# Last layer of a fused attention, expert and token-mixing kernel: ten of twelve row blocks transposed by VectorE from 512-byte gathers instead of by TensorE

## The chip, the cores and the metric

The kernel runs on one core of a Trainium2 chip. The metric is device time in microseconds (us) of one execution, lower is better. The engines are named as the profile names them: PE is TensorE (PEld its weight loads), DVE is VectorE, ACT is ScalarE, POOL is GpSimd and SP is the engine that only issues transfers.

## The reference

Three layers follow one another on a batch of 2, 768 tokens and 512 channels: windowed attention with 8 heads, a layer with 8 experts in which each token goes to one expert, and a token-mixing layer. The change concerns the way from the second layer's rows into the third layer, which computes:

```
def _moe2_ref(x, w_theta, w_tok_r, w_tok_i, w_ch):
    theta = x @ w_theta
    cos_t, sin_t = (np.cos(theta), np.sin(theta))
    zr = x * cos_t
    zi = x * sin_t
    yr = np.einsum('ts,bsd->btd', w_tok_r, zr)
    yi = np.einsum('ts,bsd->btd', w_tok_i, zi)
    y = yr + yi
    u = x + y
    return u + np.maximum(u @ w_ch, 0.0)
```

Here x is what the expert layer gives: for token s, `p[e] * (relu(x[s] @ w1[e]) @ w2[e])`.

## The kernel before

**Expert layer.** Tokens are sorted by expert into 18 slots of 128 rows. The results of a slot leave PSUM scaled (`y_rows`, and `y_last` for the last full slot, `y_few` for the last partial one) into the DRAM table `yd`, one row of 512 channels (2 KB) for each token. The index `yidx` says for each token in which row of `yd` it lies.

**Last layer.** The 1,536 tokens are 12 blocks of 128, k = 0 to 11; blocks 0 to 5 are batch entry 0. The matrix products run as three products of split operands (high and low parts), so each operand is needed twice. For a block k:

- `gather_y(k)`: POOL issues an indirect transfer (a gather) of the block's 128 rows of `yd` into the tile `yg`, tokens on partitions, for which there are four buffers.
- `h_tr(k)`: PE transposes `yg` in four 128x128 pieces into a PSUM tile `b` (channels on partitions). `h_xh` copies it on ACT into `xh` and again into `xTf`, which the end of the layer needs; `h_xl` subtracts on DVE, which gives `xl`.
- `h_theta(k)`: 12 matmuls from `xh` and `xl` with the weights `wth` give theta, in PSUM tile `th`.
- `trig_a`, `trig_s`: theta is reduced to a small angle (`kk`, `rr`) and its sine and cosine are taken, on ACT and DVE. `trig_b` multiplies them with the gathered rows (`si` on POOL, `kk` on DVE). `trig_c` splits the products into the tiles `z` (copies on ACT, one difference on POOL, one on DVE).
- `h_mix(k, d)`, d = 0 to 3: 12 matmuls each from `z` with the token-mixing weights `wtok` (`wtokr` for all but the first block of an entry), accumulated in the PSUM tiles `a`.

Block 0 goes another way: its rows are gathered before the last slot is there, and `first_put` adds that slot's rows through a second matmul with a 0/1 matrix (`hitT`); then come theta(0), a transpose back, and `y_few`'s 32 matmuls into the tile `few`.

**Order.** Everything is issued in a hand-written order, each engine works its own list in order. Block 0 to 2 are woven by hand; from k = 1 the loop runs, and in its step k PE does h_mix(k, 0), theta(k+2), the transposes of block k+3, h_mix(k, 1), h_mix(k, 2), h_mix(k, 3):

```
            h_mix(k, 0)
            gather_y(k + 4)
            ...
            h_theta(k + 2)
            h_tr(k + 3)
            h_mix(k, 1)
            ...
            trig_a(k + 2)
            h_xh(k + 3)
            trig_s(k + 2)
            h_xl(k + 3)
```

Between these, `job_tick` works off pieces of a job list, one job in a step, on DVE and ACT: table weights that arrive as 64-bit floats are turned into 32-bit ones with integer operations (`jw`, lines 402 to 414). After the last block of an entry, `h_u` adds the mixing result onto `xTf`, `h_split` splits it and `h_out` does the product with `w_ch`.

Of the kernel before, what the change touches and what calls it, by code (L numbers as in the profile page):

```python
# [12 lines left out]
I32 = mybir.dt.int32  # L13
# [35 lines left out]
YLAST = RBASE[E - 1] * 128  # L49
NRAW = 3  # L50
# [35 lines left out]
HU = 32  # L86
XL = 0
# [8 lines left out]
def f32(ap):  # L96
    return ap.bitcast(F32)


@with_exitstack  # L100
def kernel(
# [93 lines left out]
    yidx = ct([128, NB], I32, "yidx")  # L195
    erows = {}
# [249 lines left out]
    with ExitStack() as actx:  # L446
# [338 lines left out]
        def lead_out():  # L785
            A.activation(y0, head["y"], AF.Copy)
# [582 lines left out]
    with ExitStack() as mctx:  # L1369
# [64 lines left out]
        def first_put():  # L1434

            outs = first["xT"] = [pB.tile([128, 2, 128], F32, tag="b", name="first") for _ in range(2)]
            for n, (rows, pick) in enumerate(((first["rows"], ident), (first["yo"], first["hitT"]))):
                for j in range(4):
                    PE.matmul(
                        outs[j // 2][:, j % 2],  # L1440
                        lhsT=rows[:, j * 128 : (j + 1) * 128],
                        rhs=pick,
                        start=(n == 0 and j % 2 == 0),
                        stop=(n == 1 and j % 2 == 1),
                    )
# [109 lines left out]
        def mm2_few(u, out=None):  # L1555
# [33 lines left out]
        def y_rows(r, lo, hi):  # L1589
            for i in range(lo, hi):  # L1590
# [6 lines left out]
                A.activation(yo[:P, :W], yp[:P, :W], AF.Copy, scale=ps)  # L1597
# [32 lines left out]
        for u in range(64):  # L1630
# [79 lines left out]
            if 0 <= i < RTILES[r]:  # L1710
                gather_p(r, i)
            if u == HU:
                gather_p0()
# [13 lines left out]
    with ExitStack() as hctx:  # L1727
        hb = hctx.enter_context(tc.tile_pool(name="hb", bufs=2, side="right", reuse_waits="tile"))
        pA = hctx.enter_context(tc.tile_pool(name="pA", bufs=6, space=PSUM))
        x2s, xTb, zs, xps, xparts, ths, trig, acc, us = {}, {}, {}, {}, {}, {}, {}, {}, {}  # L1730

        def gather_y(k):
            if k >= NB:
                return
            yg = hb.tile([128, DM], F32, tag="yg", name="yg", bufs=4)
            G.indirect_dma_start(yg, None, yd[:], bass.IndirectOffsetOnAxis(ap=yidx[:, k : k + 1], axis=0))
            x2s[k] = yg

        def h_tr(k, pool=None):
# [3 lines left out]
            if t == 0:  # L1743
                xTb[b] = hb.tile([128, 4, S], F32, tag="xTf", name="xTf")
            tp = (pool or pB).tile([128, 4, 128], F32, tag="a" if pool else "b", name="b")
            for j in range(4):
                PE.transpose(tp[:, j], x2s[k][:, j * 128 : (j + 1) * 128], ident)
            xps[k] = tp

        def h_xh(k, both=True):  # L1750
# [5 lines left out]
            if both:  # L1756
# [28 lines left out]
        def trig_a(k, c=slice(0, DM), tick=lambda: None):  # L1785
# [9 lines left out]
            V.tensor_scalar(kk, kk, MAGIC, None, op0=ALU.subtract)  # L1795
# [16 lines left out]
        def trig_i(k, c=slice(0, DM), eng=G):  # L1812
            if k < NB:
                si = trig[k][2][:, c]
                eng.tensor_tensor(si, si, x2s[k][:, c], op=ALU.mult)  # L1815

        def trig_r(k, c=slice(0, DM)):
            if k >= NB:
                return
            kk, x2 = trig[k][0][:, c], x2s[k][:, c]  # L1820
            V.tensor_scalar(kk, kk, -2.0, 1.0, op0=ALU.mult, op1=ALU.add)
            V.tensor_tensor(kk, kk, x2, op=ALU.mult)

        def trig_b(k, c=slice(0, DM), eng=G):
# [16 lines left out]
        def trig_c(k, c=slice(0, DM), eng=G):  # L1841
# [75 lines left out]
        for k in range(1, 4):  # L1917
            gather_y(k)
        halves = (slice(0, 256), slice(256, 512))
# [67 lines left out]
        gather_y(4)  # L1987
# [4 lines left out]
        for k in range(1, NB):  # L1992
# [10 lines left out]
            gather_y(k + 4)  # L2003
# [12 lines left out]
            if k == HS:  # L2016
                h_split(0, 0, 0, S)
                h_split(0, 1, 0, S, G)
# [10 lines left out]
            if k == HS:  # L2029
                h_split(0, 2, 0, S)  # L2030
                h_split(0, 3, 0, S, G)
# [72 lines left out]
```

## Time and profile before

| what | value |
|---|---|
| three runs, median (lowest to highest) | 473.17 us (472.94 to 473.29) |
| the profiled execution's own time | 472.97 us |
| its span, from first to last instruction | 471.2 us |
| PE busy | 462.9 us, 98% of the span |
| DVE busy | 349.4 us, 74% |
| ACT busy | 254.3 us, 54% |
| POOL busy | 134.0 us, 28% |

The last layer begins at about 290 us of the span. Of the span's own time 1.8 us lie around it. [...]

### The profile page before, as it was taken

How to read it: one execution, taken by the hardware profiler on the slowest of the kernel's cores; microseconds unless marked ns; L12 is line 12 of the kernel's file. 1: busy time of each engine (PE TensorE's matmuls, PEld its weight loads, DVE VectorE, ACT ScalarE, POOL GpSimd, SP SyncE). 2: the span in 40 equal slices, each digit the busy share in tenths (PEclk: the TensorE clock that was granted, in tenths of full speed). 3: DMA queues.
4: the chain of work that ended last, by engine and by line, in shares of the span. 5: the costliest groups of instructions: out<-in, count | busy, mean ns of one | idle time of the engine just before them, and what ended most of it. 6: DMA issues, size and time to landing. Idle time of an engine off the chain costs nothing.

```text
span 471.2 us, 9456 instructions
## 1 busy us (share of the span) xinstructions
PE 462.9 (98%) x3310; PEld 382.6 (81%) x3310; DVE 349.4 (74%) x918; ACT 254.3 (54%) x613; POOL 134.0 (28%) x185
## 2 busy tenths in 40 slices
PE   8999999999999999999999999999999999999996
PEld 4677777788888898878777888888888888888885
DVE  5888889778678687878887746587999899751522
ACT  5988786722647666565754544556555355520300
POOL 8602322204041403040514302104543332430400
PEclk9999999999999999999999999999999999999999
DMA  8977577616967888888999991600023000001022
GB/s 243 370 226 255 166 250 248 231 47 197 323 181 232 281 292 272 256 255 275 310 348 298 304 321 61 207 24 22 24 73 125 12 19 19 1 33 35 34 79 93
DMA packets 60490, 82.97 MB, mean 176 GB/s; under 512 B 5608, under 2 KB 39656, under 8 KB 60440
## 3 DMA queue, kind: packets, MB, share of 16 engines
q1 hardware_dynamic: 52212, 62.06, 40.3%
q0 software_dynamic: 4272, 9.92, 6.7%
q10 hardware_dynamic: 3956, 10.36, 6.6%
q8 instruction: 27, 0.44, 0.4%
q14 instruction: 23, 0.19, 0.1%
HBM read 70.94 MB, written 11.38 MB: 175 GB/s over the span
## 4 chain that ended last, share of the span: by engine, by line
PE 86%; ACT 4%; DMA 3%; issue 3%; DVE 3%; POOL 1%; DVEq 0%; ACTq 0%; POOLq 0%
PE a L1859 21%; PE o L1547 12%; PE h L1474 8%; PE h L1491 8%; PE b L1896 7%; PE th L1783 7%; PE s L557 4%; PE x L636 3%; PE pt L612 3%; PE o L1563 2%; ACT pr L589 2%; DMA yd<-yo 2%; PE y L653 1%; PE tr L1323 1%; PE small L860 1%
## 5 line engine op out<-in xcount | busy, mean ns | idle before, releaser
L1859 PE MATMUL a<-wtokr,z 128*128 128x512 f32 x480 | 85.9, 337 | 0.0
L1859 PEld LDWEIGHTS a<-wtokr,z 128*128 128x128 f32 x480 | 73.8, 188 | 9.3
L1547 PE MATMUL o<-w2s,hh 128*128 128x512 f32 x192 | 62.9, 407 | 0.0
L589 ACT ACTIVATE pr<-sm,st 128x256 f32<-128x256 f32 (+1 forms) x96 | 46.0, 482 | 15.4 <-DVE st L579 15.3
L1491 PE MATMUL h<-xT,w1s 128*128 128x288 f32 (+3 forms) x384 | 51.9, 284 | 1.2 <-DVE w1s L1352 0.7
L1491 PEld LDWEIGHTS h<-xT,w1s 128*128 128x128 f32 x384 | 48.8, 189 | 4.4 <-DVE w1s L1352 1.1
L1456 DVE TENSOR_TENSOR w2s<-raw,w2s 128x512 fp32r<-128x512 f32 x56 | 38.4, 688 | 8.4 <-ACT w2s L1455 8.4
L579 DVE CUSTOM_DVE_ANT_0 sm<-s,bias 128x256 f32<-128x256 f32 (+1 forms) x96 | 34.0, 395 | 9.2 <-PE s L557 5.1
L1474 PEld LDWEIGHTS h<-xT,raw 128*128 128x128 f32 x256 | 37.0, 190 | 4.4 <-issue 3.9
L1474 PE MATMUL h<-xT,raw 128*128 128x192 f32 (+3 forms) x256 | 40.5, 311 | 0.0
L1547 PE MATMUL o<-w2s,hl 128*128 128x512 f32 x96 | 38.0, 396 | 0.0
L1547 PEld LDWEIGHTS o<-w2s,hh 128*128 128x128 f32 x192 | 32.3, 184 | 6.2 <-DVE w2s L1456 1.6
L1455 ACT ACTIVATE w2s<-raw 128x512 fp32r<-128x512 f32 x56 | 35.0, 628 | 2.9 <-DMA raw<-in_w_dram 1.4
L1599 POOL DMA_DIRECT2D yd<-yo x13 | 8.3, 636 | 80.3 <-ACT yo L1597 80.3
L1904 DVE SCALAR_TENSOR_TENSOR ob<-b,xTf 128x512 f32<-128x512 f32 (+1 forms) x16 | 8.8, 556 | 27.1 <-PE b L1896 24.3
L1815 POOL TENSOR_TENSOR si<-si,yg 128x512 f32<-128x512 f32 x10 | 13.5, 1346 | 50.5 <-ACT si L1808 47.5
L1352 DVE TENSOR_TENSOR w1s<-raw,w1s 128x512 fp32r<-128x512 f32 x32 | 21.9, 688 | 5.9 <-ACT w1s L1351 4.5
L557 PE MATMUL s<-kall,q 64*128 64x256 f32 (+1 forms) x192 | 26.2, 393 | 0.0
L411 ACT ACTIVATE wtokr<-jw 128x512 fp32r<-128x512 f32 x15 | 9.5, 633 | 29.4 <-DVE jw L408 29.4
L404 DVE SCALAR_TENSOR_TENSOR jw<-jraw,jw 128x512 int32<-128x512 int32 x26 | 24.7, 952 | 0.4
L406 DVE SCALAR_TENSOR_TENSOR jw<-jraw,jw 128x512 int32<-128x512 int32 x26 | 24.6, 948 | 0.2
L612 PE MATMUL pt<-ident,pr 128*128 128x128 f32 x176 | 24.6, 278 | 0.1
(289 smaller groups left out, 968.9 us busy)
## 6 DMA issues: line engine op xcount, KB each, us to landing
raw<-in_w_dram SPq DMA_DIRECT2D x60, 512.0 KB, 5.2
vv<-in_pack_dram SPq DMA_DIRECT2D x10, 512.0 KB, 5.5
jraw<-in_w_tokT_dram ACTq DMA_DIRECT2D x10, 512.0 KB, 4.5
w<-in_w_dram SPq DMA_DIRECT2D x16, 256.0 KB, 6.0
kall<-in_pack_dram SPq DMA_DIRECT2D x10, 320.0 KB, 5.0
xd<-xt SPq DMA_DIRECT2D x12, 256.0 KB, 2.2
q<-in_pack_dram SPq DMA_DIRECT2D x11, 256.0 KB, 4.4
jraw<-in_w_tokT_dram ACTq DMA_DIRECT2D x10, 256.0 KB, 4.8
```

The lines of the kernel that those rows point to most:

```text
L557: PE.matmul(sp[hh][:, 0:W], lhsT=qs[n][half, j], rhs=kall[half, b, j, t * 160 + 160 - W : t * 160 + 160], start=True, stop=True,)
L579: V.tensor_tensor_reduce(out=sm[:, hh, 0:W], in0=ust[u]["s"][hh], in1=bias[:, 2 * j + hh], scale=-0.125, scalar=BIG, op0=ALU.add, op1=ALU.min,
L589: A.activation(pr[:, hh, 0:W], sm[:, hh, 0:W], AF.Exp, bias=st[:, hh : hh + 1], scale=-1.0, accum_out=sums[n][:, 2 * j + hh : 2 * j + hh + 1],
L612: PE.transpose(pt[:, hh, c], pr[:, hh, c * 128 : (c + 1) * 128], ident)
L1455: A.activation(h2, bb[:, o], AF.Copy)
L1456: V.tensor_tensor(l2, bb[:, o], f32(h2), op=ALU.subtract)
L1474: PE.matmul(hp[:, :N], lhsT=pieces[u // 2][1][:, j, o * 128 : (o + 1) * 128], rhs=x[:, j, :N], start=(j == 0), stop=(j == 3),)
L1491: PE.matmul(hp[:, :N], lhsT=wa[:, j], rhs=xa[:, j, :N], start=(k == 0), stop=(k == 11))
L1547: PE.matmul(out[:M], lhsT=ha[:, lo : lo + M], rhs=wa, start=(f == 0 and q == 0), stop=(f == 7 and q == 2),)
L1783: PE.matmul(th, lhsT=xa[:, j], rhs=wa[:, j], start=(n == 0), stop=(n == 11))
L1859: PE.matmul(acc[b][d][o], lhsT=za[:, d * 128 : (d + 1) * 128], rhs=wa[:, lo:hi], start=(t == 0 and n == 0 and (o == 0 or d % 2 == 0)), sto ...
L1896: PE.matmul(op[:, : hi - lo], lhsT=wa[:, d, e * 128 : (e + 1) * 128], rhs=ua[d][:, lo:hi], start=(n == 0), stop=(n == 11),)
```

## The change

Four things are changed, all for the last layer.

1. The channels of a row of `yd` are stored in another order: position q*128 + j*32 + c holds channel j*128 + q*32 + c (q and j from 0 to 3, c from 0 to 31). The engines that write `yd` rows do so by a four-dimensional pattern (`by_quad`, `plain`); the narrow slots get there by the order in which `mm2_few` reads its weights.
2. For blocks 2 to 11 the transposes on PE go. POOL gathers the block a second time, now for `xq`, in four gathers of 128 pieces of 512 bytes (`gather_q`, with indices `yq` that `piece_rows` makes on DVE late in the expert layer), laid so that one DVE instruction, which transposes squares of 32 by 32, writes `xTf` whole. `xh` and `xl` are then made from `xTf`, and ACT's copy into `xTf` goes.
3. `first_put` (block 0) and `h_tr(1)` form their transposes by ordinary matmuls with 32 columns of weights each, four times as many as before.
4. POOL's multiplication and difference of each block go to DVE, also two differences of `h_split` in step 8; DVE's first operation in `trig_a` (`kk` minus a constant) goes to ACT for blocks 2 to 11.

The buffers change too: `yg` has two instead of four, `xq` has two, and the gathers of blocks 1 to 4 are listed ahead of `y_few`.

```diff
+def by_quad(ap):
+    return ap.rearrange("p (q j c) -> p j q c", q=4, c=32)
+def plain(ap):
+    return ap.rearrange("p (j q c) -> p j q c", q=4, c=32)
...
+        def piece_rows(q):
+            for i in range(4):
+                V.tensor_scalar(
+                    yq[32 * q : 32 * q + 32, i],
+                    yidx[32 * i : 32 * i + 32, VT:NB],
+                    4.0,
+                    float(q),
+                    op0=ALU.mult,
+                    op1=ALU.add,
+                )
...
                 for j in range(4):
-                    PE.matmul(
-                        outs[j // 2][:, j % 2],
-                        lhsT=rows[:, j * 128 : (j + 1) * 128],
-                        rhs=pick,
...
+                    for q in range(4):
+                        PE.matmul(
+                            outs[j // 2][32 * q : 32 * q + 32, j % 2],
+                            lhsT=by_quad(rows)[:, j, q],
+                            rhs=pick,
...
                     PE.matmul(
                         out[g * c : (g + 1) * c, : 4 * c],
                         lhsT=hx[:, :c],
-                        rhs=w[:, 4 * g * c : 4 * (g + 1) * c],
+                        rhs=w.rearrange("p (j q c) -> p q j c", q=4, c=32)[:, g * c // 32 : (g + 1) * c // 32],
...
-            V.tensor_scalar(yo, yps[E - 1][0], pslot.pop(RBASE[E - 1]), None, op0=ALU.mult)
+            V.tensor_scalar(by_quad(yo), plain(yps[E - 1][0]), pslot.pop(RBASE[E - 1]), None, op0=ALU.mult)
...
+        def gather_q(k):
+            if not VT <= k < NB:
+                return
+            xq = xqs[k] = hb.tile([128, DM], F32, tag="xq", name="xq", bufs=2)
+            for i in range(4):
+                G.indirect_dma_start(
+                    xq[:, i * 128 : (i + 1) * 128],
+                    None,
+                    yd.rearrange("n (q w) -> (n q) w", q=4),
+                    bass.IndirectOffsetOnAxis(ap=yq[:, i, k - VT : k - VT + 1], axis=0),
+                )
...
+            if k >= VT:
+                xps[k] = xTb[b][:, :, t * 128 : (t + 1) * 128]
+                V.transpose(
+                    xps[k].rearrange("p j (i a) -> p i j a", i=4),
+                    xqs.pop(k).rearrange("p (i j c) -> p i j c", i=4, j=4),
+                )
+                return
             for j in range(4):
-                PE.transpose(tp[:, j], x2s[k][:, j * 128 : (j + 1) * 128], ident)
+                for q in range(4):
+                    rows = by_quad(x2s[k])[:, j, q]
+                    PE.matmul(tp[32 * q : 32 * q + 32, j], lhsT=rows, rhs=ident, start=True, stop=True)
...
-            if both:
+            if both and k < VT:
                 h_xf(k)
...
-            V.tensor_scalar(kk, kk, MAGIC, None, op0=ALU.subtract)
+            if k < VT:
+                V.tensor_scalar(kk, kk, MAGIC, None, op0=ALU.subtract)
+            else:
+                A.activation(kk, kk, AF.Copy, bias=-MAGIC)
...
-        def trig_i(k, c=slice(0, DM), eng=G):
+        def trig_i(k, c=slice(0, DM), eng=V):
             if k < NB:
                 si = trig[k][2][:, c]
-                eng.tensor_tensor(si, si, x2s[k][:, c], op=ALU.mult)
+                eng.tensor_tensor(plain(si), plain(si), rows(k, c), op=ALU.mult)
...
-        def trig_c(k, c=slice(0, DM), eng=G):
+        def trig_c(k, c=slice(0, DM), eng=V):
...
-        for k in range(1, 4):
+        for k in range(1, 3):
             gather_y(k)
+            gather_q(k + 1)
+        gather_q(4)
+        gather_y(3)
...
-            gather_y(k + 4)
+            gather_q(k + 4)
+            gather_y(k + 3)
```

How the lists of three engines change. On PE, at the begin of the last layer, before (a row is the line, the operation and the tiles, with the shape it writes and how many follow alike):

```order
L1439 MATMUL first<-ident,rows 128x128 x4
L1439 MATMUL first<-hitT,yo 128x128 x4
L1936 MATMUL th<-wth_97,xh 128x256 x2
...
L1940 MATMUL b<-ident,xTf 128x128 x4
L1563 MATMUL few<-late,y_107 32x128 x32
L1747 MATMUL b<-ident,yg 128x128 x4
L1859 MATMUL a<-wtok_95,z_4494 128x512
```

and after the change:

```order
L1469 MATMUL first<-ident,rows 32x128 x16
L1469 MATMUL first<-hitT,yo 32x128 x16
L2002 MATMUL th<-wth_97,xh 128x256 x2
...
L2006 MATMUL b<-ident,xTf 128x128 x4
L1593 MATMUL few<-late,y_107 32x128 x32
L1804 MATMUL b<-ident,yg 32x128 x16
L1922 MATMUL a<-wtok_95,z_4561 128x512
```

Block 0 and block 1 have more and narrower matmuls, of the form that `few` has in both; the later rows `b<-ident,yg`, one of four transposes in each block from 2 to 11, are gone from the list.

On DVE, one step of the loop (step 1), before:

```order
L1795 TENSOR_SCALAR kk<-kk 128x512
L1797 SCALAR_TENSOR_TENSOR rr<-kk,th 128x512
L1799 SCALAR_TENSOR_TENSOR rr<-kk,rr 128x512
L1801 TENSOR_SCALAR rr<-rr 128x512
L1767 TENSOR_TENSOR xl<-b,xh 128x512
L402 TENSOR_SCALAR jw<-jraw 128x512
L404 SCALAR_TENSOR_TENSOR jw<-jraw,jw 128x512
L1821 TENSOR_SCALAR kk<-kk 128x512
L1822 TENSOR_TENSOR kk<-kk,yg 128x512
...
L1839 TENSOR_TENSOR z_4785<-kk,z_4784 128x512
```

and after the change:

```order
L1795 STREAM_TRANSPOSE xTf<-xq 128x4x4x32
L1857 SCALAR_TENSOR_TENSOR rr<-kk,th 128x512
L1859 SCALAR_TENSOR_TENSOR rr<-kk,rr 128x512
L1861 TENSOR_SCALAR rr<-rr 128x512
L1824 TENSOR_TENSOR xl<-xTf,xh 128x512
...
L1878 TENSOR_TENSOR si<-si,yg 128x512
L1884 TENSOR_SCALAR kk<-kk 128x512
L1885 TENSOR_TENSOR kk<-kk,yg 128x512
...
L1902 TENSOR_TENSOR z_4842<-si,z_4841 128x512
L1902 TENSOR_TENSOR z_4840<-kk,z_4839 128x512
```

The transpose stands where the subtraction of the constant stood, and two operations are added, `si<-si,yg` and `z<-si,z`.

On POOL, from the begin of the last layer, before:

```order
L1736 DMA yg<-yd,yidx 128x512 x4
L1815 TENSOR_TENSOR si<-si,yg 128x512
L1839 TENSOR_TENSOR z_4680<-si,z_4679 128x512
L1736 DMA yg<-yd,yidx 128x512
L1815 TENSOR_TENSOR si<-si,yg 128x512
```

and after the change:

```order
L1771 DMA yg<-yd,yidx 128x512
L1780 DMA xq<-yd,Lall 128x128 x4
L1771 DMA yg<-yd,yidx 128x512
L1780 DMA xq<-yd,Lall 128x128 x8
L1771 DMA yg<-yd,yidx 128x512
L1780 DMA xq<-yd,Lall 128x128 x4
```

(`Lall` is the memory in which the indices `yq` lie.) POOL has only gathers left until the end of the loop, five for a block instead of one.

## Rows read from the trace of the kernel before

**Rows 1.** The page: busy time, share of the span and instructions by engine.

```profile
PE 462.9 (98%) x3310; PEld 382.6 (81%) x3310; DVE 349.4 (74%) x918; ACT 254.3 (54%) x613; POOL 134.0 (28%) x185
```

**Rows 2.** Chain that ended last, from 285 us: start, length, what.

```profile
by line: PE a L1859 53.6%; PE b L1896 17.8%; PE th L1783 16.6%; PE b L1747 2.7%; PE th L1936 1.6%; PE o L1547 1.5%; PE first L1439 1.1%; PE few L1563 1.0%; PE h L1474 1.0%; PE b L1940 0.2%; DVE ob L1904 0.2%; PE tr L1431 0.1%; issue 0.0%
...
329.44 0.44 PE b L1747 x4
...
341.01 0.44 PE b L1747 x4
```

**Rows 3.** Timeline of PE in one step: start, length, line, operation, tiles.

```profile
340.85 0.60 PE L1747 MATMUL b<-ident,yg 128*128 128x128 f32 x4
341.20 8.58 PE L1859 MATMUL a<-wtokr,z 128*128 128x512 f32 x48
```

**Rows 4.** Timeline of PE, ACT and DVE where the last layer begins.

```profile
289.53 1.05 PE L1439 MATMUL first<-ident,rows 128*128 128x128 f32 x8
290.54 1.16 PE L1439 MATMUL first<-hitT,yo 128*128 128x128 f32 x8
...
295.16 1.69 PEld L1563 LDWEIGHTS few<-late,y 128*32 128x32 f32 x64 [0.17 <-issue]
297.05 0.42 PEld L1747 LDWEIGHTS b<-ident,yg 128*128 128x128 f32 x4 [0.20 <-issue]
297.55 2.46 PE L1859 MATMUL a<-wtok,z 128*128 128x512 f32 x12
297.74 0.60 ACT L1754 ACTIVATE xh<-b 128x512 fp32r<-128x512 f32 x1 [0.25 <-PE b L1747]
299.91 0.76 PEld L1783 LDWEIGHTS th<-wth,xh 128*128 128x128 f32 x4 [0.22 <-DVE xl L1767]
310.19 0.42 DVE L1815 TENSOR_TENSOR si<-si,yg 128x256 f32<-128x256 f32 x1
312.83 2.24 PE L1859 MATMUL a<-wtokr,z 128*128 128x512 f32 x12
```

**Rows 5.** Timeline of DVE in one step, and one later row.

```profile
344.20 0.42 DVE L1795 TENSOR_SCALAR kk<-kk 128x512 f32<-128x512 f32 x1
...
347.49 1.68 DVE L404 SCALAR_TENSOR_TENSOR jw<-jraw,jw 128x512 int32<-128x512 int32 x1
...
350.15 1.79 DVE L406 SCALAR_TENSOR_TENSOR jw<-jraw,jw 128x512 int32<-128x512 int32 x1
...
352.65 0.69 DVE L1839 TENSOR_TENSOR z<-kk,z 128x512 fp32r<-128x512 f32 x1
...
354.05 0.42 DVE L1795 TENSOR_SCALAR kk<-kk 128x512 f32<-128x512 f32 x1
...
375.43 0.68 DVE L406 SCALAR_TENSOR_TENSOR jw<-jraw,jw 128x512 int32<-128x512 int32 x1
```

**Rows 6.** Timeline of POOL: first gathers of the layer, then one step.

```profile
293.29 0.95 POOL L1736 DMA_INDIRECT yg<-yd,yidx  x1 [5.30 <-DMA yd<-yo]
294.54 0.95 POOL L1736 DMA_INDIRECT yg<-yd,yidx  x1 [0.30 <-issue]
...
306.52 0.94 POOL L1736 DMA_INDIRECT yg<-yd,yidx  x1 [9.78 <-DMA yd<-y]
...
347.27 1.34 POOL L1815 TENSOR_TENSOR si<-si,yg 128x512 f32<-128x512 f32 x1 [4.32 <-ACT si L1808]
349.54 1.85 POOL L1839 TENSOR_TENSOR z<-si,z 128x512 fp32r<-128x512 f32 x1 [0.92 <-ACT z L1834]
351.54 1.26 POOL L1736 DMA_INDIRECT yg<-yd,yidx  x1 [0.16 <-issue]
```

**Rows 7.** The view of tile yg: its gathers, from issue to landing.

```profile
DMA to landing us min/median/max: 3.3/3.6/5.0
```

**Rows 8.** DVE's small copies and an idle time late in the expert layer.

```profile
264.67 0.61 DVE L1411 COPY sidx<-toks 32x1 int32<-32x1 int32 x4
267.82 0.69 DVE L1456 TENSOR_TENSOR w2s<-raw,w2s 128x512 fp32r<-128x512 f32 x1 [2.54 <-ACT w2s L1455]
```

More of the change, by code (lines that the diff above doesn't have):

```diff
@@ L49 @@
 YLAST = RBASE[E - 1] * 128
+VT = 2
 NRAW = 3
@@ L86 @@
 HU = 32
+QIDX = (50, 52, 54, 56)
 XL = 0
@@ L195 @@
     yidx = ct([128, NB], I32, "yidx")
+    yq = Lall.rearrange("p k e -> p (k e)")[:, 0 : 4 * (NB - VT)].bitcast(I32).rearrange("p (i k) -> p i k", i=4)
     erows = {}
@@ L785, in lead_out @@
         def lead_out():
-            A.activation(y0, head["y"], AF.Copy)
+            A.activation(by_quad(y0), plain(head["y"]), AF.Copy)
         cp = rt([128, 2, 8], "cp")[:, 0]
@@ L1438, in first_put @@
                 for j in range(4):
-                    PE.matmul(
-                        outs[j // 2][:, j % 2],
-                        lhsT=rows[:, j * 128 : (j + 1) * 128],
-                        rhs=pick,
-                        start=(n == 0 and j % 2 == 0),
-                        stop=(n == 1 and j % 2 == 1),
-                    )
+                    for q in range(4):
[3 more added lines that the diff above has]
+                            rhs=pick,
+                            start=(n == 0 and j % 2 == 0),
+                            stop=(n == 1 and j % 2 == 1),
+                        )
         wsp2 = {}
@@ L1596, in y_rows @@
                 yp = yps[r][i]
-                A.activation(yo[:P, :W], yp[:P, :W], AF.Copy, scale=ps)
+                if c == 128:
+                    A.activation(by_quad(yo[:P]), plain(yp[:P]), AF.Copy, scale=ps)
+                else:
+                    A.activation(yo[:P, :W], yp[:P, :W], AF.Copy, scale=ps)
                 n = (RBASE[r] + i) * 128
@@ L1711 @@
                 gather_p(r, i)
+            if u in QIDX:
+                piece_rows(QIDX.index(u))
             if u == HU:
@@ L1729 @@
         pA = hctx.enter_context(tc.tile_pool(name="pA", bufs=6, space=PSUM))
[L1730 removed]
+        x2s, xqs, xTb, zs, xps, xparts, ths, trig, acc, us = {}, {}, {}, {}, {}, {}, {}, {}, {}, {}
         def gather_y(k):
@@ L1794, in trig_a @@
             tick()
-            V.tensor_scalar(kk, kk, MAGIC, None, op0=ALU.subtract)
+            if k < VT:
+                V.tensor_scalar(kk, kk, MAGIC, None, op0=ALU.subtract)
+            else:
+                A.activation(kk, kk, AF.Copy, bias=-MAGIC)
             tick()
@@ L1810, in trig_s, with rows @@
             A.activation(kk[:, c], kk[:, c], AF.Square)
-        def trig_i(k, c=slice(0, DM), eng=G):
+        def rows(k, c):
+            return by_quad(x2s[k])[:, c.start // 128 : c.stop // 128] if k else plain(x2s[k][:, c])
+        def trig_i(k, c=slice(0, DM), eng=V):
             if k < NB:
                 si = trig[k][2][:, c]
-                eng.tensor_tensor(si, si, x2s[k][:, c], op=ALU.mult)
+                eng.tensor_tensor(plain(si), plain(si), rows(k, c), op=ALU.mult)
         def trig_r(k, c=slice(0, DM)):
@@ L1819, in trig_r, with trig_b @@
                 return
-            kk, x2 = trig[k][0][:, c], x2s[k][:, c]
+            kk = trig[k][0][:, c]
             V.tensor_scalar(kk, kk, -2.0, 1.0, op0=ALU.mult, op1=ALU.add)
-            V.tensor_tensor(kk, kk, x2, op=ALU.mult)
-        def trig_b(k, c=slice(0, DM), eng=G):
+            V.tensor_tensor(plain(kk), plain(kk), rows(k, c), op=ALU.mult)
+        def trig_b(k, c=slice(0, DM), eng=V):
             trig_i(k, c, eng)
@@ L2017 @@
                 h_split(0, 0, 0, S)
-                h_split(0, 1, 0, S, G)
+                h_split(0, 1, 0, S)
             h_mix(k, 2)
@@ L2030 @@
                 h_split(0, 2, 0, S)
-                h_split(0, 3, 0, S, G)
+                h_split(0, 3, 0, S)
             if HS < k < HS + 4:
```

4 lines of the change are left out of this document (2 added, 2 removed).

## Prediction

> **What bounds the kernel now.** I read the page first: PE is busy for 98% of the span, the others for 74% or less [rows 1]. A share alone proves little, so next comes the chain of work that ended last, in order of time. From 285 us on it never leaves PE but for the last 0.4 us: mixing, theta, transposes and the product with `w_ch` follow one another [rows 2]. So in the last layer PE is the limit, and work taken from PE's list comes off the end, as long as no other engine is late with what PE reads next. The loop's period is 11.57 us (341.01 minus 329.44, [rows 2]), and every one of its steps has it. The timeline of DVE then shows how near the next engine is: it went from one step's first operation to the next one's in 354.05 minus 344.20 = 9.85 us [rows 5], faster than PE, so it runs ahead until the `z` buffers stop it.
>
> **Taken from PE: the transposes of blocks 2 to 11.** They started at 340.85, and the mixing behind them at 341.20: 0.35 us from start to start [rows 3]. Ten blocks make 3.5 us. The chain gives 0.44 us for the same four [rows 2], since it counts from end to end and the small matmul behind a large one ends late; 4.4 us is the upper bound. I take 0.35, because what moves is the start of the matmul behind.
>
> **Added to PE: block 1 and block 0.** Narrow matmuls, 32 columns of weights and 128 moving, have rows of their own shape: `few`, whose 64 weight loads took 1.69 us, 0.026 each, after 0.17 us that nothing explains, and the next wide ones started after another 0.20 [rows 4]. I read these as the price of changing between the narrow and the wide form. The program's list has 32 matmuls there, so one listed is two in the trace. Block 1 gets 16, in the trace 32: 32 x 0.026 = 0.83 us, right behind `few` and so without the first change, from 296.85 (295.16 + 1.69) to 297.68, and mixing starts at 297.88 instead of 297.55 [rows 4]: +0.33. If instead the rows of block 1 land only at 297.05, it is +0.53. Behind that stands a second chain: ACT's `xh` starts when the transposes end (297.74 before), and theta(1) waited for the `xl` that follows [rows 4]; it moves by about as much. I take +0.4, bounds 0.2 and 0.6. Block 0's two groups took 1.01 us (290.54 minus 289.53) and 1.16 [rows 4]; narrow they are 2 x 32 x 0.026 = 1.7 and two changes of form, 2.1. The second group can't begin before DVE has written the last slot, so I count nothing (bounds -0.2 and +0.2).
>
> **Moved to DVE.** In a step it loses one pass of 0.42 us (`kk`) and gains two that cost 0.69 each, as the like difference at 352.65 [rows 5]. It also loses a wait: the two integer operations took 1.68 and 1.79 us where POOL's own two ran beside them (347.27 and 349.54, [rows 6]), and 0.68 where POOL did nothing of the kind (375.43, [rows 5]). With POOL's passes gone that gives back 1.00 + 1.11 us. A 32-square transpose of 128x512 stands in no row. It reads one operand and writes one; the cheapest such pass is 0.42 us, the dearest pass of that size in the trace 1.85 (POOL, [rows 6]); I take 0.69, the usual price of a 128x512 pass on this engine. The step becomes 9.85 - 0.42 - 2.11 + 1.38 + 0.69 = 9.4 us, between 9.1 and 10.55. PE's step becomes 11.57 - 0.35 = 11.22. So DVE stays hidden, and nothing is charged; a transpose would have to cost 2.5 us before it counted. ACT changes one pass for another, the copy into `xTf` for the subtraction, both beside PE. DVE even gets a start: block 2's `xl` had to wait for PE's transposes behind h_mix(0, 1), and now waits for a gather only.
>
> **Moved to POOL.** Five gathers for a block instead of one. A gather took 0.95 us with 0.30 to the next while DVE was little used, and 1.26 in the loop [rows 6]; five are 6.3 to 7.8 us, below 11.22. A gather lands 3.6 us after issue (3.3 to 5.0, [rows 7]). With two `xq` buffers, the gathers for block k+4 start when block k+2 is transposed, two DVE steps before they are needed: hidden. The store of `y_few` now stands behind the gathers of blocks 1 to 4, the last of which waits for a `yg` buffer that DVE frees with the products of block 1, near 313 us (they began at 310.19, [rows 4]); all later gathers wait for that store, as one did before (306.52, [rows 6]). SP has nothing urgent behind it. With 3.6 us for that gather and as much for the store, the round for block 5 begins at about 320 and lands at 320 + 4 x 1.26 + 3.6 = 329. DVE wants it in step 2, whose first operation stood at 344.20 - 9.85 = 334.4 [rows 5] and now comes some 2 us earlier. A wait of a few us there would be DVE's and not PE's, since DVE is ahead of PE by then.
>
> **Small edits.** `piece_rows` puts 16 small operations of some 0.15 us (0.61 for four, [rows 8]) on DVE in the expert layer, 2.4 us in four places; DVE has gaps like the 2.54 us at 267.82 [rows 8], and they are charged at nothing (2.4 us if that cover were gone). The new order of a row's channels changes patterns of ACT, DVE and of the weights that `mm2_few` reads, not counts: nothing, for runs of 32 elements stay whole.
>
> **Sum.** -3.5 + 0.4 + 0 = -3.1 us. The profiled execution's 472.97 becomes 469.87; the median of the runs lies 0.20 above it, so 470.1. By the bounds: -4.4 + 0.2 - 0.2 = -4.4, thus 468.8, and -3.5 + 0.6 + 0.2 = -2.7, thus 470.5.
>
> **Rivals.** *Block 3 arrives late.* At the layer's begin POOL now has ten gathers before block 3 is whole: 293.29 + 9 x 1.25 = 304.5, landed at 308.2; with 1.56 each and 5.0 to landing, 312.3. DVE's transpose of block 3 stands in its list ahead of the first products of block 1, which began at 310.19 and which PE needs at 312.83 [rows 4]. I expect DVE there at about 308, so nothing is lost; at the bad end z(1) comes 2 us late and PE waits some 1.5 us: 471.6. *POOL's gathers become the bound.* Their time rose from 0.95 to 1.26 when DVE was busy [rows 6]. If each had to wait for two more DVE passes of 0.69, five would be 13.2 to 14.7 us; from 11.22 / 5 = 2.24 us each it decides. At 13.2 a step loses 2 us, some seven steps 14, of which the lead of DVE over PE (two steps at 11.2 less 9.4) pays about 4: +10 - 3, thus 480, slower. [...] *The transpose costs over 2.5 us.* DVE then sets the step: at 3.5 us 12.2, and 1.0 us a step for eight steps less the lead: 477. Nothing speaks for it but that no row has the operation. *PE gains nothing*, since a wait takes the place of the transposes, say theta's weights or PSUM: 473.5. Against it: the chain has no gap at these places.
>
> **How the numbers follow.** Forecast, all hidden: 0.72 (own range 468.8 to 471.0). Block 3 late: 0.11. PE gains nothing: 0.06. Gathers bound: 0.07. Transpose too dear: 0.04. The first two are faster by over 0.2%, which is about what a measurement of this kernel can tell from none: 0.83. The third is the same, 0.06, the last two slower, 0.11. The range of 8 in 10 takes in the first two: 468.9 to 471.9.
>
> **What would show it.** Right: the period in the chain is 11.2 us; the narrow matmuls of block 1 have about 0.03 us from start to start; DVE's integer operations all take 0.7 us, and its step, where it isn't stopped, 9 to 10; a gather takes at most 1.3 us; PE shows no wait at mixing or theta. Wrong: PE's timeline has idle time before `z` or `xl`, DVE waits for `xq`, or the period is above 11.3.

## The result: 468.95 us, 4.3 us less, and what the profile after shows

The changed kernel took 468.95 us (median of 4 runs, 468.41 to 468.99), the kernel before beside it 473.23 (472.94 to 473.75): ratio 0.9906, 95% interval 0.9888 to 0.9923. The forecast was 470.1 in a range of 468.9 to 471.9, so the time lies at its very end. `transpose_x3` and the last three groups of experiments below were run later, and in all of them, unchanged kernels too, engines stood still near the layer's begin, so those runs are compared within their own group alone.

The page's row of engines, answering to [rows 1]:

```profile
PE 458.3 (98%) x3346; PEld 379.0 (81%) x3346; DVE 348.4 (75%) x956; ACT 257.5 (55%) x613; POOL 140.9 (30%) x203
```

The chain that ended last, in order of time (start, length, what), at the layer's begin and in the loop, answering to [rows 2]:

```profile
289.46 1.53 PE first L1469 x48
...
291.45 3.07 PE th L2002 x24
...
294.96 1.88 PE few L1593 x64
296.85 0.12 issue
296.97 1.08 PE b L1804 x32
298.05 2.32 PE a L1922 x12
300.37 2.96 PE th L1840 x12
...
325.59 2.79 PE th L1840 x12
328.38 8.33 PE a L1922 x48
336.71 2.79 PE th L1840 x12
```

The same chain of before at the layer's begin:

```profile
289.69 2.00 PE first L1439 x16
...
291.72 3.07 PE th L1936 x24
...
295.23 1.88 PE few L1563 x64
...
300.01 2.97 PE th L1783 x12
```

From 291.45 us on PE is still the whole chain, but for the last 0.42 us, DVE's `ob`, as before. The period is 336.71 minus 325.59 = 11.12 us, not the 11.22 of the prediction: a block's transposes were worth 0.44 or 0.45. Over ten blocks that is 4.4 to 4.5. Against it stand block 1 with +0.63 (from the start of `few` to theta(1): 300.37 - 294.96 = 5.41, and 300.01 - 295.23 = 4.78 before) and block 0 with nothing (first to theta(0): 291.45 - 289.46 = 1.99, and 2.03 before).

The timeline of DVE in one step, answering to [rows 5], that of POOL, answering to [rows 6], and the view of tile `xq`, answering to [rows 7]:

```profile
331.04 0.70 DVE L1795 STREAM_TRANSPOSE xTf<-xq 128x512 f32<-128x512 f32 x1
...
334.48 0.69 DVE L421 SCALAR_TENSOR_TENSOR jw<-jraw,jw 128x512 int32<-128x512 int32 x1
...
339.96 0.70 DVE L1795 STREAM_TRANSPOSE xTf<-xq 128x512 f32<-128x512 f32 x1
```

```profile
319.79 1.24 POOL L1780 DMA_INDIRECT xq<-yd,Lall  x1 [5.85 <-DMA yd<-y]
...
333.55 1.38 POOL L1780 DMA_INDIRECT xq<-yd,Lall  x1 [0.31 <-DVE rr L1861]
```

```profile
DMA to landing us min/median/max: 2.5/2.7/6.0
```

DVE's step is 339.96 - 331.04 = 8.92 us, the transpose 0.70, the integer operations 0.69. The longest gather takes 1.38, and the round behind the store begins at 319.79, where the prediction put it (320); 2.7 us to landing beside 3.6 for `yg`.

### The profile page after: what moved, and what is told of

It is laid out like the page before. It is cut to its first block, busy times and chain, and to the rows that moved or that the text cites. A ratio compares the mean times of both kernels' runs of the same rounds, so it can differ in the third digit from the quotient of the medians.

```text
span 467.1 us, 9581 instructions
## 1 busy us (share of the span) xinstructions
PE 458.3 (98%) x3346; PEld 379.0 (81%) x3346; DVE 348.4 (75%) x956; ACT 257.5 (55%) x613; POOL 140.9 (30%) x203
## 4 chain that ended last, share of the span: by engine, by line
PE 85%; ACT 4%; DVE 3%; issue 3%; DMA 2%; POOL 1%; DVEq 0%; ACTq 0%; POOLq 0%
PE a L1922 21%; PE o L1577 12%; PE h L1504 8%; PE h L1521 8%; PE b L1959 7%; PE th L1840 7%; PE s L574 4%; PE x L653 3%; PE pt L629 3%; PE o L1593 2%; ACT pr L606 2%; DMA yd<-yo 2%; PE y L670 1%; PE tr L1340 1%; ACT ps L638 1%
## 5 line engine op out<-in xcount | busy, mean ns | idle before, releaser
L1780 POOL DMA_INDIRECT xq<-yd,Lall x40 | 41.6, 1040 | 26.7 <-issue 10.4
L653 PE MATMUL x<-ps,vv 128*64 128x128 f32 x352 | 24.5, 279 | 0.0
L1556 ACT ACTIVATE hh<-h 128x256 fp32r<-128x256 f32 (+2 forms) x32 | 11.8, 370 | 20.4 <-PE h L1521 19.9
```

Source lines behind the costliest of these rows:

```text
L653: PE.matmul(xp[64 * hh : 64 * hh + 64, j], lhsT=vv[:, i, h * 64 : (h + 1) * 64], rhs=ps[:, hh, c], start=(c == 0), stop=(c == nch - 1),)
L1780: G.indirect_dma_start(xq[:, i * 128 : (i + 1) * 128], None, yd.rearrange("n (q w) -> (n q) w", q=4), bass.IndirectOffsetOnAxis(ap=yq[:, i ...
```

## The experiments

**What the transposes of a block cost PE: `twice` and `one_of_four`.** Both are the kernel before with another number of transposes in blocks 2 to 11.

```diff
-            for j in range(4):
-                PE.transpose(tp[:, j], x2s[k][:, j * 128 : (j + 1) * 128], ident)
+            for n in range(2 if k > 1 else 1):
+                for j in range(4):
+                    PE.transpose(tp[:, j], x2s[k][:, j * 128 : (j + 1) * 128], ident)
```

> The kernel before, with the four transposes of blocks 2 to 11 done twice over (the second time into the same place). Theory A: the change's gain in the loop is TensorE's own time for the transposes, 0.107 us each and 0.44 a block, and nothing else; then four more cost 0.43 a block, the period rises from 11.57 to 12.00 us and the time by 4.3 to 477.5. Theory B: the transposes cost 0.35 a block, as the prediction had it, and the other 0.09 came from what was moved between VectorE and GpSimd; then the period is 11.92 and the time 476.7.

`one_of_four` does one of the four for k > 1 and reads its result in place of all:

```diff
-            for j in range(4):
+            n = 4 if k < 2 else 1
+            for j in range(n):
                 PE.transpose(tp[:, j], x2s[k][:, j * 128 : (j + 1) * 128], ident)
-            xps[k] = tp
+            xps[k] = tp if n == 4 else tp[:, 0:1].to_broadcast([128, 4, 128])
```

> The kernel before, with one transpose instead of four for blocks 2 to 11, whose result is read in place of all four (this leaves out three quarters of the transposed rows); VectorE, ScalarE and GpSimd do as much as before. Theory A: three transposes of 0.107 us less in each of ten blocks, period 11.25 us, time 470.0. Theory B: 3 x 0.0875, period 11.31, time 470.6. Theory C, the gain needs VectorE's and GpSimd's part: period 11.57, 473.2.

Measured: 477.39 us (ratio 1.0102, interval 1.0077 to 1.0127) and 469.11 (0.9935, 0.9910 to 0.9960). The chain of `twice`, then that of `one_of_four`:

```profile
330.22 0.87 PE b L1748 x8
...
342.22 0.87 PE b L1748 x8
```

```profile
338.65 0.11 PE b L1748
...
349.88 0.11 PE b L1748
```

The periods are 12.00 and 11.23 us, beside 11.57 with four transposes and 11.12 with none. Each transpose costs 0.11 us wherever the count goes, so four cost 0.44 from end to end. Theory A holds twice, by the periods; the two times alone, with their intervals, would also fit the 476.7 and 470.6 of theory B.

**Who does the products: `dve_products` and `pool_products`.** The first is the kernel before with POOL's products and differences on DVE, the second the changed kernel with them back on POOL.

```diff
-        def trig_i(k, c=slice(0, DM), eng=G):
+        def trig_i(k, c=slice(0, DM), eng=V):
...
-        def trig_c(k, c=slice(0, DM), eng=G):
+        def trig_c(k, c=slice(0, DM), eng=V):
...
-                h_split(0, 1, 0, S, G)
+                h_split(0, 1, 0, S)
...
```

> The kernel before, with GpSimd's products and differences (and the two of step 8) on VectorE, nothing else changed. Theory A: VectorE's step falls from 9.85 to about 9.1 us, but the period stays 11.57 us and the time 473.2, since VectorE was hidden. Theory B: the period falls to 11.48 and the time by 0.9 to 472.3.

> The changed kernel, with the products and differences back on GpSimd, which then does five gathers and two passes for a block. Theory A: all of it hides, the period stays 11.13 us and the time 469.0; GpSimd needs some 9.7 us a step. Theory B: the period rises to 11.22, the time to 469.9. Theory D: GpSimd's list gets too long or its passes wait for gathers that wait for buffers, TensorE waits for z, over 470.5.

Measured: 472.51 us (0.9995, 0.9985 to 1.0005) and 470.00 (0.9951, 0.9933 to 0.9969). In `dve_products` DVE's step, from one `xl` to the next, fell from 9.85 to 8.83 us although it does two more passes:

```profile
335.02 0.68 DVE L1767 TENSOR_TENSOR xl<-b,xh 128x512 fp32r<-128x512 f32 x1
343.85 0.68 DVE L1767 TENSOR_TENSOR xl<-b,xh 128x512 fp32r<-128x512 f32 x1
```

So POOL's two passes had cost DVE about 9.85 + 1.38 - 8.83 = 2.4 us a step, and it cost no time, since PE is the bound. `pool_products` tells when it does. Its DVE step is 10.37 us, 0.76 below PE's, and yet PE waited once, at the change of batch entry:

```profile
375.23 2.02 PE L1922 MATMUL a<-wtok,z 128*128 128x256 f32 x10 [0.56 <-DVE xTf L1934]
```

`h_u` of batch entry 0 reads the accumulators that block 6's mixing needs. It is extra work for DVE, most of it in one step (some 3 us between 363 and 374 us in the changed kernel), for which a step of 10.37 has no room. The period stays 11.13 us, so theory B falls, although its 469.9 lies nearest. The wait of 0.56 us accounts for the 0.5 between the profiled executions (469.50 and 468.99); the medians lie 1.05 apart, and what the rest is isn't shown.

**The order of a row's channels: `interleave_wide` and `interleave_narrow`.** The changed kernel with position 4*m + j for channel j*128 + m, so that neighbouring channels of a 128-block lie 16 bytes apart; the first with wide transposes for blocks 0 and 1, the second with narrow ones as in the change.

```diff
-    return ap.rearrange("p (q j c) -> p j q c", q=4, c=32)
+    return ap.rearrange("p (q c j) -> p j q c", j=4, c=32)
...
```

> The changed kernel with another order of a row's channels: position 4*m + j holds channel j*128 + m (m from 0 to 127). A 512-byte piece holds the same channels as in the change, but each 128-channel group is now one pattern of single stride 4, so that blocks 0 and 1 can be transposed by wide operations as before the change. Theory A: block 1 has cost 0.63 us over before by its narrow matmuls and the changes of form; this comes back, time 468.3, mixing starts 0.5 us after block 1's first transpose. Theory E: strides of 16 bytes cost on the way (weight loads of rows, the moving weights of the narrow slots, VectorE's and ScalarE's passes), the time stays at 469 or rises.

> The changed kernel with the same other order of channels (position 4*m + j), but blocks 0 and 1 by narrow matmuls as in the change. Theory A: 469.0, no row gets longer. Theory E: ScalarE's or VectorE's passes, the narrow slots' matmuls or the 32-square transposes get longer by their strides of 16 bytes; over 469.5.

Measured: 486.33 us (1.0299, 1.0274 to 1.0325) and 485.48 (1.0273, 1.0246 to 1.0299). Groups by shape (count, busy time, mean ns of one) of `interleave_narrow`, then the same of the changed kernel:

```profile
L1795 DVE STREAM_TRANSPOSE xTf<-xq 128x512 f32<-128x512 f32 x10 | 10.9, 1093 | 0.0
L1878 DVE TENSOR_TENSOR si<-si,yg 128x512 f32<-128x512 f32 x10 | 10.8, 1082 | 1.4 <-ACT si L1868 1.4
L1593 PE MATMUL few<-late,y 128*32 128x128 f32 x64 | 3.8, 404 | 0.0
```

```profile
L1795 DVE STREAM_TRANSPOSE xTf<-xq 128x512 f32<-128x512 f32 x10 | 7.0, 705 | 0.0
L1878 DVE TENSOR_TENSOR si<-si,yg 128x512 f32<-128x512 f32 x10 | 6.9, 685 | 1.4 <-ACT si L1868 1.4
```

An operand read at 16-byte steps cost DVE 1.08 instead of 0.69 us, the transpose 1.09 instead of 0.70; ACT's `yo`, written at such steps, rose from 0.68 to about 1.2, and a narrow matmul of 128 moving columns, whose neighbours are read 512 bytes apart here, from 0.27 to 0.40 (the 64 of `few` together from 2.0 to 3.8). Most of the 16.5 to 17.4 us was lost in the expert layer, where the narrow slots' 192 matmuls took 427 ns in the median instead of 285: the last layer began near 302 instead of 289.5. Theory E holds, and what wide transposes of blocks 0 and 1 would give back can't be read beside it. The change's own order, which keeps runs of 32 elements whole, cost nothing of this: ACT's `yo` takes 0.68 us before and after it.

**One narrow group more: `narrow_2`.** The changed kernel with block 2 on PE as well.

```diff
-VT = 2
+VT = 3
```

> The changed kernel with block 2 too by narrow matmuls on TensorE instead of gathers and VectorE. Theory A: 32 times 0.026 us and two changes of form (0.17 and 0.20), 1.2 us more than the change, 470.2. Rival, the narrow form only costs its 0.83 us: 469.8. Rival, it hides behind waits at the layer's begin: 469.0.

Measured: 470.64 us (0.9959, 0.9944 to 0.9974), 1.7 more than the changed kernel. The chain shows the group, and that it isn't alone:

```profile
304.69 1.05 PE b L1804 x32
...
325.49 0.64 ACT xh L1811
326.17 3.06 PE th L1840 x12
```

The narrow group takes 1.05, block 1's took 1.08; beyond it the chain runs over ACT and DVE from 305.77 to 326.17, where theta(4) waits for `xh`. So the 1.7 us aren't the group's alone. That DVE starts later when a block's rows come from PE is read from this chain and not tested.

**DVE's transpose made dearer: `transpose_x6` and `transpose_x3`.** The changed kernel with the transpose written six times and three times.

```diff
-                V.transpose(
...
+                xq = xqs.pop(k)
+                for _ in range(6):
+                    V.transpose(
...
```

> The changed kernel with each 32-square transpose on VectorE done six times over. Theory A: VectorE's step of 8.92 us grows by 5 x 0.63 to 12.1, over TensorE's 11.13; it becomes the limit in the steps that have a job, about seven: 0.95 us each less the lead it has at the begin (3 us), so 472 to 474, with waits of TensorE before z, xl or the accumulators. Rival, VectorE has more slack than its busy rows show: 469.0.

Measured: 493.84 us (1.0445, 1.0419 to 1.0472), far above the 472 to 474 of the theory. DVE's timeline, and the longest waits of PE's weight loads in the loop (us in total, times, longest):

```profile
342.09 4.44 DVE L1797 STREAM_TRANSPOSE xTf<-xq 128x512 f32<-128x512 f32 x6
```

```profile
PEld th L1842 <- ACT xh L1813: 11.8, 8, 2.3
...
PEld a L1924 <- DVE xTf L1936: 4.2, 1, 4.2
PEld a L1924 <- ACT z L1899: 4.0, 1, 4.0
```

One transpose takes 0.74 us there, DVE's step 12.9, and the waits sum to 20 us. The granted clock is lower there too: 0.92 of full speed from 289 to 330 us and 0.97 from 330 to 430, where the changed kernel has 1.00 in both. PE waits for block 2's `xh` at 307.54 us already, and 4.0 us for z(1) at 316.34, so the lead of two steps that the prediction gave DVE wasn't there to pay.

> The changed kernel with DVE's 32-square transpose of blocks 2 to 11 written three times instead of once; nothing else. Two passes of 0.745 us more make DVE's unstopped step 8.92 + 1.49 = 10.4 us, still below PE's 11.13. Theory A (the prediction's sentence that a transpose has to cost 2.5 us in all, so that DVE's step passes PE's, before it counts; here it costs 2.2): no wait of PE for xTf or xl in the loop, 468.95 us, 468.6 to 469.4. Theory B (DVE already counts below that, at the change of batch entry, where the first mixing of block 6 needs the accumulators that DVE's reads free, as in the run with the products on POOL, whose DVE step was 10.37): one wait of PE of 0.5 to 1 us for a tile that DVE writes near 375 us and 469.4 to 470.2.

Measured: 484.92 us (1.0244, 1.0221 to 1.0267). Neither theory: most of it is the standstill that the next groups are about. Behind it, with a DVE step of 10.65 us, PE waits 2.1 us for `xh` at 339.03 and 1.3 us for DVE's `xTf` at the change of batch entry, at 390.42, so theory B's wait is there too.

**More gathers, and block 1 off PE: `gathers_x2` and `block_1_by_dve`.** The first gathers each 512-byte piece a second time into a spare tile; the second has `VT = 1`, gathers listed by need and h_mix(0, 1) ahead of theta(1).

```diff
+            for i in range(4):
+                more = hb.tile([128, 128], F32, tag="more", name="more", bufs=2)
+                G.indirect_dma_start(
+                    more,
...
```

```diff
-VT = 2
+VT = 1
...
+        h_mix(0, 1)
...
         h_theta(1)
...
-        h_mix(0, 1)
...
```

> The changed kernel in which POOL gathers each of the four 512-byte pieces of a block a second time, into a tile that nobody reads: nine gathers a block instead of five, at 0.94 to 1.38 us each 8.5 to 12.4 us a step beside PE's 11.13. Theory A (gathers are hidden as long as POOL's step stays below PE's, and the lead of DVE and the two buffers cover an excess of under 1 us a step): 468.95, 468.6 to 469.6. Theory B (the rival of the prediction: issuing beside a busy DVE gets dearer, a gather takes 2 us or more): DVE waits for xq, PE for z, 475 or more. Between them, if a gather takes 1.3 to 1.4: 11.7 to 12.6 a step, 0.6 to 1.5 us late a step, of which the lead pays most: 469.5 to 473. Also right under A: the layer's first blocks come later, since 9 gathers more stand ahead of block 3; if that is seen, PE waits at z(1) or xl(3).

> The changed kernel with block 1 too taken from PE: its rows are gathered in 512-byte pieces and transposed by DVE, the first mixing of block 0 comes right behind the few matmuls and theta(1) after it, and POOL's first gathers are listed by need. PE loses the narrow group of block 1, 1.01 us from start to start, against which the change of form behind few (0.2) stays. Theory A (PE is the bound here too, and a gather of block 1 lands while the first mixing of block 0 runs): 0.6 to 0.8 less, 468.2, 467.9 to 468.5. Theory B (the four small gathers and DVE's transpose, split and products of block 1 are late for theta(1), or for the sine of block 1 that mixing needs behind block 0): PE waits 0.8 us or more between 300 and 315 us, 469.0 or more.

Measured: 504.92 to 517.29 us in four runs, slower but too far apart for a price, and 484.18 (1.0227, 1.0200 to 1.0254). In `gathers_x2` nine gathers took 382.13 - 368.91 = 13.22 us, 1.47 each with the waits for the spare tile, which is above PE's 11.13, and DVE then waits in each step:

```profile
368.91 0.94 POOL L1780 DMA_INDIRECT xq<-yd,Lall  x1 [0.30 <-issue]
...
382.13 0.94 POOL L1780 DMA_INDIRECT xq<-yd,Lall  x1 [0.30 <-issue]
```

```profile
364.35 0.71 DVE L1803 STREAM_TRANSPOSE xTf<-xq 128x512 f32<-128x512 f32 x1 [1.58 <-DMA xq<-yd,Lall]
```

That is the condition of the prediction's rival of gathers as the bound, 13.2 us a step, at twice its gathers. Its price of 10 us isn't seen: PE's steps stay 11.13 us (theta starts at 359.15, 370.27 and 381.40), and PE waits for DVE at the change of batch entry alone, 3.0 us in all. How much of that is owed to the time that PE had lost before isn't shown.

`transpose_x3` and both kernels of this group also lost some 11 to 22 us at one place, from about the 40th of `few`'s narrow matmuls on, and `gathers_x2` lost some 16 us more in the loop. From 413.8 to 435.8 us PE does the wide matmuls of mixing and theta a few at a time there, and again waits for nothing that the profile shows ("issue"), until POOL's gathers end:

```profile
421.30 1.01 PE L1930 MATMUL a<-wtokr,z 128*128 128x512 f32 x4 [0.69 <-issue]
...
427.69 1.07 PE L1930 MATMUL a<-wtokr,z 128*128 128x512 f32 x2 [1.73 <-issue]
```

```profile
432.26 0.95 POOL L1771 DMA_INDIRECT yg<-yd,yidx  x1 [0.30 <-issue]
```

POOL had issued gathers since 342.61 with no pause above 1.3 us, and for the first 70 us of that PE showed no such gaps.

**Whose standstill it is: `after_again`, `transpose_x3_again`, `block_1_again`.** The changed kernel unaltered, and two of the edits again.

> The changed kernel once more, unaltered, beside the two that follow. Theory A (the standstill of PE at few in the three runs before belongs to their edits): 468.95, 468.4 to 469.6, no standstill. Theory B (it comes from a state of the chip in that session, since PE's list up to there is the same in all): if the state is still there, 478 to 482 with PE standing still from about the 40th matmul of few; if it is gone, no kernel of this call has it.

> The kernel with three transposes on DVE again. Theory A (the standstill belongs to the edit): 484 to 486 as before. Theory B (session): without it, 469.0 if a DVE step of 10.4 us below PE's 11.13 costs nothing, as the prediction had it, or 469.4 to 470.4 with one wait for a tile of DVE near 375 us if the change of batch entry already feels it.

> The kernel with block 1 too by gathers and DVE, again. If the standstill belongs to the session and is gone: 0.6 to 0.8 us under the changed kernel of this call, so about 468.2, if the rows of block 1 are there in time; at or above the changed kernel if PE waits for them or for z(1). If the standstill belongs to the edit: 483 to 486.

Measured: 481.49 us (1.0143, 1.0123 to 1.0163), 484.52 (1.0207, 1.0188 to 1.0227) and 485.38 (1.0222, 1.0204 to 1.0239), the kernel before 474.49. So the standstill isn't the edits' own: the unaltered changed kernel has it, and is there slower than the kernel before. Nor does the chip alone decide: `pool_products`, with the same first row of gathers, had run at 470.00 on the chip (number 12) of `transpose_x3`. Against `after_again` three transposes cost 3.0 us (PE's two waits in `transpose_x3` make 3.4), and taking block 1 from PE costs 3.9 instead of giving 0.7; its first row has fourteen gathers, the last of them at 309.62 beside 304.53 in `after_again`. What they cost or give without a standstill stays open.

**What makes PE stand still: `before_again`, `after_third`, `few_later`, `gathers_later`.** The two kernels unaltered; `few` moved behind POOL's first gathers; nine of the first fifteen gathers moved behind `few`. The diffs of the last two:

```diff
...
         h_mix(0, 2)
+        next(few)
+        next(few)
         h_theta(2)
+        next(few, None)
```

```diff
-        for k in range(1, 3):
-            gather_y(k)
-            gather_q(k + 1)
-        gather_q(4)
-        gather_y(3)
+        gather_y(1)
+        gather_q(2)
+        gather_y(2)
...
         next(few, None)
+        gather_q(3)
+        gather_q(4)
+        gather_y(3)
```

> The kernel before, unaltered. If the state of the last two calls is still there: 474 to 475, and by theory A (a long row of narrow matmuls beside POOL's gathers) a short standstill in few, 1 to 2 us, since only 3 gathers of POOL lie beside it; by theory B (PE's list of instructions at a fixed place) none in few. If it is gone: 472.8 and none.

> The changed kernel, unaltered, to tell the state of this call: 481 to 482 with PE standing still in few if it is there, 468.4 to 469.6 if not.

> The changed kernel with few's 64 narrow matmuls moved from ahead of block 1's transposes to ahead of theta(2), behind the first gathers, into a PSUM buffer of the other pool; two more changes of form on PE, +0.4, and nothing to cover the landing of block 1's rows, +0.5 to +2. Theory A (narrow rows beside gathers): in the state, 32 narrow matmuls of block 1 stay beside the gathers and pass, few runs at full rate behind them: 469.5 to 472. Theory B (a fixed place of PE's list, some 90 instructions behind the transposes of block 0): the standstill stays, now in the first mixing or theta(1), 480 or more. Without the state: 469.5 to 471.5.

> The changed kernel with POOL's gathers of xq for blocks 3 and 4 and of yg for block 3 listed behind y_few's store instead of ahead of it: 6 gathers instead of 15 beside few and block 1. Theory A, in the state: PE's standstill ends when the sixth gather is issued, near 301 instead of 307, but the rows of block 3 land only near 316, DVE's transpose of them comes late and PE waits for z(1) or xl(3) instead: 475 to 481 with the standstill 6 us shorter. Theory B: standstill as long as in after_third. Without the state: 469 plus the wait for block 3, 472 to 478.

Measured: 474.71 us (0.9992, 0.9979 to 1.0006), 483.72 (1.0200, 1.0160 to 1.0240), 484.74 (1.0225, 1.0194 to 1.0256) and 479.44 (1.0098, 1.0079 to 1.0117), the kernel before 475.05. PE and POOL in `after_third`:

```profile
294.91 1.50 PE L1593 MATMUL few<-late,y 128*32 128x128 f32 x42
297.30 0.38 PE L1593 MATMUL few<-late,y 128*32 128x128 f32 x2 [0.89 <-issue]
...
307.31 0.44 PE L1593 MATMUL few<-late,y 128*32 128x128 f32 x2 [1.48 <-issue]
```

```profile
304.39 0.94 POOL L1780 DMA_INDIRECT xq<-yd,Lall  x1 [0.30 <-issue]
```

PE passes 42 narrow matmuls in 1.50 us, then one to four at a time, with starts 1.4 or 2.1 us apart, and no wait that the profile shows. When this ends follows POOL in each kernel: here at 307.3, 2.9 us after the start of the last gather of its first unbroken row of ten. In `gathers_later`, whose sixth and last gather of the row starts at 299.90, PE is free at 302.04, and in `before_again`, with three gathers, the last at 295.73, at 297.52:

```profile
302.04 1.31 PE L1593 MATMUL few<-late,y 128*32 128x128 f32 x20 [0.31 <-issue]
```

```profile
297.52 0.63 PEld L1563 LDWEIGHTS few<-late,y 128*32 128x32 f32 x21 [1.20 <-issue]
```

`gathers_x2`, with eighteen, agrees (314.92 and 318.54). In `few_later` PE passes block 1's narrow matmuls unhindered, and ACT stands instead, with the last gather at 304.95:

```profile
308.02 0.60 ACT L1811 ACTIVATE xh<-b 128x512 fp32r<-128x512 f32 x1 [10.01 <-remote]
```

So theory A holds in that the standstill ends with POOL's unbroken row of gathers, and falls in that narrow rows are what it strikes: here it was ACT, in the loop of `gathers_x2` it was wide matmuls, and the time came out as theory B had it. A long row of gathers alone isn't enough for it either, as the 70 us in `gathers_x2` show. Theory B's mechanism, a fixed place in PE's list, falls with that and with the 1.2 us in `before_again`. `gathers_later` lost on the other side what theory A named: z(1) came late, and PE waited 0.96 us for it at 321.29. On top comes the clock: in `after_third` the granted clock is 0.65 from 296 to 307 us, 0.50 from 307 to 309 and 0.82 from 309 to 320, where the first profile has 1.00; mixing's first twelve matmuls take 3.81 us in the chain, from 309.68 on, instead of 2.32.

What the engines lack is not shown. A few matmuls at a time, with no wait for another engine, made the author think of a shortage of instructions. But the page of the changed kernel's first profile, which has no standstill, and that of `transpose_x3`, which has one, list the same loads of the instruction queues: 27 on one, 0.44 MB, so 16 KB each, and 25 of 8 KB on another. One of the 27 ran between 292 and 294 us in the first, and between 294 and 296 in `transpose_x3`, both near the begin of `few`, and the next came at about the same place of PE's list: between 304 and 306 us, and between 314 and 318 in `transpose_x3`, whose PE is some 11 us behind. So these loads don't tell the two apart, and no run here shows that instructions were short. Nor is it shown why the same list ran through in the first profile, with POOL's gathers at the same place.

## Why the prediction was right in kind and off in size

- **PE is the bound, and transposes come off the end.** Right: no wait of PE at mixing or theta in the profile after, and `twice` and `one_of_four` move the time by the same price.
- **0.35 us a block, "because what moves is the start of the matmul behind".** This is the step that failed. From the start of the transposes to the start of the mixing it is 0.35 [rows 3], but the first mixing matmul behind them is slowed: it lasts 0.48 us, and 0.40 after the change. PE in the step before and after the change, from mixing's start to theta's: 349.62 - 341.20 = 8.42 before and 336.55 - 328.22 = 8.33 after.

```profile
341.20 8.58 PE L1859 MATMUL a<-wtokr,z 128*128 128x512 f32 x48
349.62 2.02 PE L1783 MATMUL th<-wth,xh 128*128 128x512 f32 x8
```

```profile
328.22 8.49 PE L1922 MATMUL a<-wtokr,z 128*128 128x512 f32 x48
336.55 2.02 PE L1840 MATMUL th<-wth,xh 128*128 128x512 f32 x8
```

  The 0.09 us a block are hidden behind the next row's start, and the chain's 0.44 [rows 2], named as the upper bound, was the price. Ten times 0.09 is 0.9 of the 1.2 us by which the forecast was off.
- **Block 1, +0.4.** Measured +0.63, just past the bound of 0.6: there are 0.12 us of waiting ahead of the group at 296.97, and theta(1) followed. That is probably the late landing that the prediction priced at +0.53: the profile names no releaser here, but in `narrow_2` the chain names the gather of block 1 at this place. Block 0: nothing, as said.
- **The sum.** -4.5 + 0.63 - 0.04 = -3.9; the spans differ by 4.1. The 0.2 that is left lies ahead of the layer, which began 0.23 earlier; the runs of this study with the expert layer of before began it between 288.6 and 289.7, so that is no more than scatter. The prediction's "own range" ends at 471.0, where its bounds add up to 470.5.
- **DVE's step, 9.4.** 8.92, below the range of 9.1 to 10.55: POOL's passes had cost DVE 2.4 us a step, not 2.11. The transpose was 0.70 for 0.69.
- **"A transpose would have to cost 2.5 us before it counted."** Too high, as far as the runs tell: with a step of 10.37, which a transpose of 2.15 would give, PE already waited in `pool_products`, and with three transposes in 2.20 us it waited at the same place in `transpose_x3`, though there behind a standstill. The price of a step isn't the only limit; the step with `h_u` in it has some 3 us more to do.
- **POOL.** Five gathers took 339.96 - 332.29 = 7.7 us between the rows of `yg`, within 6.3 to 7.8, hidden. The rival of block 3 didn't come: its last piece was issued at 304.62 and DVE transposed it at 307.72, near the 308 named. A gather took 1.38 us at most, for 0.94 at the shortest, just past the 1.3 that the prediction named as a sign; in `gathers_x2`, from 342 to 395 us, it was 1.38 at most too, and the nine of a step took 1.47 each with the waits for the spare tile. What makes a gather longer no run shows.
- **What the prediction didn't see.** It asked what slows POOL's gathers, never what a long row of them does to the others. In the later groups the changed kernel took 481.5 and 483.7 us, 12.5 and 14.8 more than at first, and the gain was a loss.

## What to carry to other kernels

Price work taken from the engine that bounds by the end of what comes behind it (the chain, or the same stretch with and without it), not by the start of the next row: here 0.09 of a block's 0.44 us lay behind the start of the large matmul that followed. DVE with a step 0.8 us below the bound wasn't hidden here, since one step carried some 3 us of extra work: PE waited 0.56 us. And where a change multiplies the gathers that one engine issues in a row, look at what stands still beside that row: six in a row instead of ten gave 4.3 us back where the engines stood.

## What the runs showed of the hardware that wasn't expected

- With one operand read at steps of 16 bytes a 128x512 pass took DVE 1.08 us instead of 0.69, and with the moving operand read at steps of 512 bytes 64 narrow matmuls took 3.8 us instead of 2.0 (`interleave_narrow`).
- A 32-square transpose of 128x512 fp32 cost DVE 0.70 us, where its other 128x512 passes of two operands took 0.65 to 0.69 in the step from 331.04; written six times over, 0.74 each (`transpose_x6`).
- In some executions engines went on by a few instructions at a time, with starts 0.7 (`gathers_later`) to 2.1 us (`after_third`) apart and no wait that the profile shows, beside an unbroken row of POOL's gathers, until 1.8 (`before_again`) to 3.6 us (`gathers_x2`) after the last one started. Narrow matmuls (`after_third`), wide ones (`gathers_x2`, up to 1.73 us idle) and ACT (`few_later`, 10.01 us idle) were struck. PE's granted clock was 0.50 from 307 to 309 us in `after_third`. Not every such row did it all the time: in `gathers_x2` PE showed no such gaps for the first 70 us of one.
